# DeltaNet and a PReLU feed-forward on one core: the banks of two solves, one row step, two banks of the ninth chunk and the shape of the last stores

## The chip, the core and the metric

The kernel runs on one core of a Trainium2 chip. Its engines work through their own instruction streams and meet through semaphores: TensorE (PE in the profile) multiplies matrices and writes into PSUM, eight banks of 512 fp32 values per partition; VectorE (DVE) and ScalarE (ACT) read those banks; GpSimd (POOL) computes in SBUF alone; SyncE (SP) issues most DMA transfers. The metric is the device time of one execution in microseconds (us). A profiled execution also has a span, from its first to its last instruction, which is a little shorter.

## The reference

Two blocks follow one another. The first is the delta rule for 4 batches and 8 heads, 768 tokens, 48 dimensions a head:

```python
k_n = k / (np.linalg.norm(k, axis=-1, keepdims=True) + 1e-06)
state = np.zeros((B, H, D, D))
for t in range(S):
    y[:, :, t] = einsum('bhd,bhde->bhe', q[:, :, t], state)
    v_old = einsum('bhde,bhd->bhe', state, k_n[:, :, t])
    state = state + beta_t * einsum('bhd,bhe->bhde', k_n[:, :, t], v[:, :, t] - v_old)
```

Its output, taken as 3072 tokens of 384 values, goes through a feed-forward layer:

```python
h = x @ w_in                                          # 384 -> 2048
g = np.maximum(h, 0.0) + alpha * np.minimum(h, 0.0)
out = g @ w_out                                       # 2048 -> 384
```

All data is fp32. The output array has one row of 384 values (1536 bytes) for each token, batch after batch.

## The kernel before, in words

**Chunks and steps.** The sequence is cut into 12 chunks of 64 tokens (NCH). A step is one chunk of one pair of batches, so there are 24 steps (N), two for each chunk. Within a chunk the recurrence becomes a triangular system: its matrix is made of products of keys (grams), its inverse is found block by block on VectorE (eliminate), and each step then needs a few groups of small matmuls.

**What a step does.** through_state (L801) multiplies the keys with the state and with the queries; the right-hand side r is made of its first part (L825) and the masked matrix a_t of its second (L508). query (L789) multiplies queries and state; ScalarE copies the result as y (L799). between_1 and between_2 (L773, L776, matmuls at L747) make the off-diagonal block of the inverse, with copies by ScalarE (L759). solve (L914, matmuls at L917) multiplies the inverse with r, and VectorE scales it to u (L921). outputs (L926, L930) adds to y (L936), next_state (L940, L946) updates the state (L954). flips (L441, transposes at L430) turn keys and queries of later steps, to_ffn (L962, L969) turns y into the input of the feed-forward layer.

**Banks.** Two banks, p_ffn, belong to the feed-forward layer; until step 15 the other six form three pairs, p_pair. ps_big() (L76) hands out the pairs in turn. From step LATE = 16 on there are two pairs and two more single banks, p_more (L1998); the single banks are then ffn_banks[0] to [3].

**Order of the work.** The instructions of all engines stand in the order in which the program issues them. Steps 4 and 5 are written out in attention (L1454), from step JOINED = 6 on a step is three bursts (burst_a, turn_round, burst_b), each followed by a stretch (L1973) in which weave (L1437) mixes pieces of three streams: the feed-forward layer of earlier chunks (tail), the elimination of later blocks, and small work put off. Each stream gets positions evenly spread between its starting point and 1: the feed-forward pieces from 0, the pieces of the elimination from 0.3. How many of each a stretch takes stands in FILL and PIECES_OF (L1989 to L1995) for steps 6 to 8. A piece of the elimination in its middle part is a row step, one multiply (L565) and one add (L571) on VectorE, from 30 to 240 elements wide.

**The feed-forward layer.** Chunks 2 to 7 take w_in in ffn_in (L1066): groups of matmuls (L1075) into the two p_ffn banks in turn, then a relu on ScalarE (L1085) and two instructions on VectorE (L1087) that free the bank. Their w_out is done by ffn_out_fast (L1128) as seven products of half size, each ended by an add on VectorE (L1160). The ninth chunk (FAST_IN = 8, counted from 0) is the first to take ffn_in_fast (L1262) and ffn_out_faster (L1367): eight pairs of columns, each with its own bank of ffn_banks[0] to [2] and its shared products in p_more, then seven products again, in a list of banks at L1397.

**Stores.** store (L1098) writes the 128 rows of an o_sb tile, 32 for each batch, to four places of the output, one transfer a batch, on SyncE's queue; in the last chunk every other one goes on ScalarE's. The last chunk stores three times: half of the tokens in full rows of 1536 bytes, then the left halves of the others (768 bytes), and, behind the last product and its add (L1425), their right halves. Then the program waits for all transfers (L2069).

Of the kernel before, what the change touches and what calls it, by code (L numbers as in the profile page):

```python
# [32 lines left out]
C = 64  # L33
# [5 lines left out]
FAST_IN = 8  # L39
# [4 lines left out]
def kernel(  # L44
# [11 lines left out]
    nc = tc.nc  # L56

    B, H, S, D = q.shape
    DM = H * D
    DFF = moe_w_in.shape[1]  # L60
    NCH = S // C
# [12 lines left out]
    doubles, big, ffn_banks = ExitStack(), [], []  # L74

    def ps_big():  # L76

        big.append(big.pop(0))
        return big[-1]
# [211 lines left out]
    for t in range(2):  # L291
# [7 lines left out]
        out=quarter_of, in_=ident.rearrange("p (t q e) -> p q t e", t=2, q=NQ4),  # L299
# [11 lines left out]
        out=picked, in0=minus.rearrange("p (q c) -> p q c", c=LB),  # L311
# [154 lines left out]
    def now(pieces):  # L466
        for x in pieces:
            x()
# [628 lines left out]

    def store(c, u, o_sb, cols=slice(0, DM)):  # L1098

        for b in range(B):  # L1100
            tok = b * S + c * C + 32 * u
            queue = nc.scalar if c == NCH - 1 and b % 2 else nc.sync
            queue.dma_start(out=out[tok : tok + 32, cols], in_=o_sb[32 * b : 32 * b + 32, cols])

    def ffn_out(c, together=False):

# [155 lines left out]
    def ffn_in_fast(c):  # L1262
        xt = xts[c]
        gss[c] = [act_of(c, i) for i in range(FP)]
        due = due_of[c] = Due()
        t = spare()[2]

        def x(k, u):
            return xt[:, k, u * 128 : (u + 1) * 128]

        def quarter(flat):
            return flat.rearrange("p (i e) -> p i e", e=128)

        def terms(i):

            if i % 2 == 0:
                return spare()[1]
            if "block" not in held:
                held["block"] = work.tile([128, HB * (HB + 1)], FP32, name="block", bufs=1)
            return quarter(held["block"][:, 0:512])  # L1280

        def pair(i):
            p = ffn_banks[i % 3]
            q = quarter(ffn_banks[2 if i == 0 else 3])
            z, g = terms(i), act_of(c, i)
            if "less" not in held:
                held["less"] = work.tile([128, G, 128], FP32, name="k_t", bufs=EARLY + 1)
            r = held["less"] if i % 2 == 0 else quarter(held["block"][:, 512:1024])
            r = r.rearrange("p (f u) e -> p f (u e)", f=2)

            def w(k, f):
                return w_in[:, k, (2 * i + f) * 128 : (2 * i + f + 1) * 128]

            def s(x):
                return input_sum(x, i // 4)[:, i % 4]

            def whole(f):
                nc.tensor.matmul(  # L1298
                    p[:, f * 256 : f * 256 + 256], w(2, f), xt[:, 2], start=True, stop=False
                )  # L1300

            def more(j, a, b):
                nc.tensor.matmul(  # L1303
                    p[:, j * 128 : j * 128 + 128], a, b, start=False, stop=(j > 0)
                )

            def shared(j, a, b):
                nc.tensor.matmul(q[:, j], a, b, start=True, stop=True)  # L1308

            def own():  # L1310
                whole(0)
                yield
                more(0, w(1, 0), x(1, 0))
                more(1, w(0, 1), x(1, 1))
                yield
                whole(1)
                yield
                more(2, w(1, 1), t[:, 3])
                yield

            def common():
                shared(0, w(0, 0), x(0, 0))
                shared(1, s(1), t[:, 1])
                yield
                shared(2, s(2), t[:, 2])
                shared(3, s(0), t[:, 0])
                nc.scalar.copy(z, q)  # L1327
                for dst, a, b in (
                    (z[:, 1], z[:, 0], z[:, 1]), (z[:, 2], z[:, 1], z[:, 2]),
                    (z[:, 1::2], z[:, 1:3], z[:, 3:4].to_broadcast([128, 2, 128])),  # L1330
                ):
                    nc.gpsimd.tensor_tensor(out=dst, in0=a, in1=b, op=ALU.add)  # L1332
                yield

            def total():
                h = g.rearrange("p f i -> p (f i)")
                nc.vector.tensor_tensor(
                    out=h, in0=p, in1=z.rearrange("p i e -> p (i e)"), op=ALU.add
                )

            def below():
                nc.scalar.activation(r, g, ACT.Relu, scale=-1.0)  # L1342

            def slope():
                for f in range(2):
                    nc.vector.scalar_tensor_tensor(  # L1346
                        out=g[:, f], in0=r[:, f], scalar=al_t[:, 2 * i + f : 2 * i + f + 1],
                        in1=g[:, f], op0=ALU.mult, op1=ALU.add,
                    )

            due.put(PER * (i + 1) + {0: PER, FP - 1: 2}.get(i, 3), total)
            due.put(PER * (i + 2) + {FP - 2: 1, FP - 1: -4}.get(i, 2), below)
            due.put(PER * (i + 2) + {FP - 2: 1, FP - 1: -2}.get(i, 5), slope)
            for gen in (own(), common()) if i == 0 else (common(), own()):
                for _ in gen:
                    due.step()
                    yield

        early = operand_sums(0)
        due.put(PER * 6 + 5, lambda: next(early, None))  # L1360
        rest = chain(early, operand_sums(1))
        for at in (6, 6, 7, 7, 8, 9, 10):
            due.put(PER * FP + at, lambda: next(rest, None))
        for i in range(FP):
            yield from pair(i)

    def ffn_out_faster(c):  # L1367

        gss.pop(c)
        due = due_of.pop(c)  # L1370
        o = [work.tile([128, DM], FP32, name="o_sb") for _ in range(2)]
        left, right_ = slice(0, DM // 2), slice(DM // 2, DM)
        u = [work.tile([128, DM // 2], FP32, name=f"u{i}", bufs=1) for i in (2, 3)]

        def operand(f, u):
            return lambda i: act[:, i, f, u * 128 : (u + 1) * 128]

        def sum_(x):
            return lambda i: sums[:, i, x]

        def weight(f, v):
            return lambda i: w_half[:, i, f, v]

        def w_sum_(x):
            return lambda i: w_sum(i, x)

        def add(to, x, p):
            nc.vector.tensor_tensor(out=to, in0=x, in1=p, op=ALU.add)

        def some(p, x, w, which):  # L1390
            for i in which:
                nc.tensor.matmul(p, x(i), w(i), start=(i == 0), stop=(i == FP - 1))  # L1392
                if i % 2 == 1:
                    due.step()
                    yield

        p = [ffn_banks[i][:, 0 : DM // 2] for i in (3, 2, 0, 3, 2, 1, 3)]  # L1397
        a = (p[0], operand(0, 0), weight(0, 0))
        b = (p[1], operand(1, 0), weight(1, 0))
        yield from some(*a, range(FP - 2))  # L1400
        yield from some(*b, range(FP - 2))
        yield from some(*a, range(FP - 2, FP))
        nc.scalar.copy(u[0], p[0])
        yield from some(*b, range(FP - 2, FP))
        add(o[0][:, left], u[0], p[1])
        yield from some(p[2], operand(1, 1), w_sum_(3), range(FP))
        assert not due.left
        yield from some(p[3], sum_(1), w_sum_(1), range(FP))
        add(u[0], u[0], p[3])
        yield from some(p[4], lambda i: act[:, i, 0, 128:256], w_sum_(2), range(FP))  # L1410
        add(u[1], u[0], p[4])
        add(o[1][:, left], u[1], p[2])
        yield from some(p[5], sum_(0), w_sum_(0), range(FP))
        add(o[0][:, right_], u[0], p[5])
        add(o[1][:, right_], u[1], p[5])
        store(c, 1, o[1])
        last = c == NCH - 1
        if last:
            store(c, 0, o[0], left)
        yield from some(p[6], sum_(2), weight(1, 1), range(FP - 2))  # L1420
        if c + 1 < NCH:
            assert c + 1 in whole
            token_sums(c + 1)
        yield from some(p[6], sum_(2), weight(1, 1), range(FP - 2, FP))
        add(o[0][:, right_], o[0][:, right_], p[6])  # L1425
        store(c, 0, o[0], right_ if last else slice(0, DM))
# [27 lines left out]
    def attention(n):  # L1454
# [2 lines left out]
        now(through_state(n))  # L1457
        now(between_1(n + 1))
        yield
        now(solve(n))  # L1460
        now(grams(n + EARLY))
        now(between_2(n + 1))
# [517 lines left out]
    for n in range(NJ, JOINED):  # L1980
# [7 lines left out]
    assert next(late, None) is None  # L1988
    PIECES_OF = {  # L1989
        JOINED: (3, WHOLE - 2 * PIECES - 6 - 2 * share - 3, 2 * PIECES),  # L1990
        JOINED + 1: (0, 4, 7), JOINED + 2: (4, 5, 5),
    }
    TURNS = [(3, 3, 4), (3, 3, 4), (4, 4, 4), (0, 5, 6)]
    FILL = {JOINED: (8, 12, 12), JOINED + 1: (10, 12, 10), JOINED + 2: (8, 10, 12)}
# [79 lines left out]
```

## Time and profile before

| | |
|---|---|
| runs shown | 646.87, 647.69, 648.09 us (median 647.69) |
| profiled execution | 648.95 us |
| its span | 647.2 us |
| granted TensorE clock | 0.997 |
| TensorE busy | 635.0 us (98%) |
| VectorE busy | 482.9 us (75%) |
| ScalarE busy | 258.6 us (40%) |
| written to memory | 4.72 MB |
| issue to landing of a store, median | 1.6 us |

A line of the timeline gives the start in us, the duration, the engine with the line of the kernel, the operation, the tile it writes and the tiles it reads, the shapes and the number of instructions merged; in brackets stand the idle time before it and what ended it. SPq and ACTq are the issues of DMA transfers on SyncE's and ScalarE's queues: the time is that of the issue, not of the data. In the view of the DMA queues each queue has its packets, its megabytes and the time its packets took as a share of 16 engines over the window.

### The profile page before, as it was taken

What the parts mean: (1) busy time and instruction counts of PE and PEld (TensorE: products, weight loads), DVE (VectorE), ACT (ScalarE), POOL (GpSimd) and SP (SyncE); (2) the same over time, 40 slices, a digit from 0 to 9 for tenths busy, and PEclk for the clock granted to TensorE, in tenths of its full rate; (3) what the DMA queues carried; (4) which work ended last, traced back from release to release, by engine and by line L of the source; (5) the groups of instructions that cost most, each with busy time, mean ns of one, the idle gap of its engine ahead of it and who ended that gap; (6) DMA issues with size and microseconds to landing.
All of it is one profiled execution on the core that took longest, in us unless ns stands there. A gap on an engine that the chain in (4) does not pass through costs nothing.

```text
span 647.2 us, 21391 instructions
## 1 busy us (share of the span) xinstructions
PE 635.0 (98%) x9177; PEld 562.7 (87%) x9177; DVE 482.9 (75%) x1160; ACT 258.6 (40%) x605; POOL 125.3 (19%) x248
## 2 busy tenths in 40 slices
PE   8899999999999999999999999999999999999997
PEld 7677787567889989989989989989999999999997
DVE  5858689978998788578678577678868568477383
ACT  6667664245553253254154144034045054042240
POOL 7267610010001000000000010000044053062360
PEclk9989999999999999999999999999999999999999
DMA  8668755113511320311210211211221210100000
GB/s 131 169 160 240 208 129 129 23 29 64 99 25 29 76 50 3 69 37 23 60 27 17 46 32 26 41 40 22 43 42 19 54 23 2 39 2 3 25 0 26
DMA packets 106799, 36.89 MB, mean 57 GB/s; under 512 B 99872, under 2 KB 103088, under 8 KB 106704
## 3 DMA queue, kind: packets, MB, share of 16 engines
q1 hardware_dynamic: 104832, 35.03, 25.0%
q8 instruction: 72, 1.18, 0.8%
q10 hardware_dynamic: 1872, 0.49, 0.4%
q14 instruction: 23, 0.19, 0.1%
HBM read 30.78 MB, written 4.72 MB: 55 GB/s over the span
## 4 chain that ended last, share of the span: by engine, by line
PE 86%; DVE 8%; issue 2%; ACT 2%; POOL 1%; DMA 1%; SPq 0%; POOLq 0%; DVEq 0%; ACTq 0%
PE p_ffn L1075 24%; PE p_ffn L1140 17%; PE p_more L1392 8%; PE p_more L1308 5%; PE p_ffn L1118 4%; PE p_ffn L1298 3%; PE p_ffn L1392 3%; PE p_ffn L1303 2%; PE p_pair L430 2%; PE p_pair L807 2%; PE p_pair L747 2%; PE p_pair L486 2%; PE p_pair L930 2%; PE p_pair L917 2%; PE p_pair L795 1%
## 5 line engine op out<-in xcount | busy, mean ns | idle before, releaser
L1075 PE MATMUL p_ffn<-xt,w_in 128*128 128x256 f32 x768 | 177.5, 384 | 0.7 <-DVE act L1087 0.5
L1075 PEld LDWEIGHTS p_ffn<-xt,w_in 128*128 128x128 f32 x768 | 142.0, 190 | 21.5 <-issue 1.5
L1085 ACT ACTIVATE act<-p_ffn 128x512 f32<-128x512 f32 x56 | 33.3, 595 | 80.4 <-PE p_ffn L1075 80.2
L1087 DVE SCALAR_TENSOR_TENSOR act<-act,al_t,p_ffn 128x256 f32<-128x256 f32 x112 | 48.5, 474 | 20.0 <-ACT act L1085 19.7
L1332 POOL TENSOR_TENSOR k_t<-k_t 128x128 f32<-128x128 f32 (+1 forms) x48 | 29.9, 623 | 167.5 <-ACT k_t L1327 165.0
L571 DVE TENSOR_TENSOR block<-block,prod 128x30 f32<-128x30 f32 (+9 forms) x150 | 50.0, 333 | 5.2
L565 DVE TENSOR_TENSOR prod<-block 128x30 f32<-128x30 f32 (+9 forms) x150 | 49.0, 327 | 4.2 <-POOL block L555 2.7
L419 POOL TENSOR_TENSOR beta_t<-beta_t,rec 128x8 f32<-128x8 f32 x20 | 5.1, 257 | 235.2 <-DVE rec L413 219.3
L1140 PE MATMUL p_ffn<-w_out,act 128*128 128x192 f32 x288 | 49.6, 328 | 0.0
L973 ACT COPY xt<-p_pair 128x384 f32<-128x384 f32 x22 | 10.4, 478 | 91.2 <-PE p_pair L969 77.5
L1140 PEld LDWEIGHTS p_ffn<-w_out,act 128*128 128x128 f32 x288 | 46.6, 190 | 0.3
L1332 POOL TENSOR_TENSOR block<-block 128x128 f32<-128x128 f32 (+1 forms) x48 | 28.0, 583 | 16.0 <-ACT block L1327 13.5
L1298 PE MATMUL p_ffn<-xt,w_in 128*128 128x256 f32 x96 | 28.7, 381 | 0.5 <-DVE o_sb L1160 0.5
L759 ACT COPY inv<-p_pair 32x256 f32<-32x256 f32 x40 | 14.5, 361 | 24.9 <-DVE u L921 24.1
L1160 DVE TENSOR_TENSOR o_sb<-u,p_ffn 128x192 f32<-128x192 f32 x24 | 7.9, 351 | 20.5 <-PE p_ffn L1140 20.0
L799 ACT COPY y<-p_pair 128x384 f32<-128x384 f32 x22 | 10.5, 479 | 31.1 <-PE p_pair L795 29.5
L1346 DVE SCALAR_TENSOR_TENSOR act<-block,al_t,act 128x256 f32<-128x256 f32 x32 | 19.1, 638 | 4.7 <-ACT block L1342 4.7
L1327 ACT COPY k_t<-p_more 128x512 f32<-128x512 f32 x16 | 9.4, 587 | 31.7 <-PE p_more L1308 27.9
L825 DVE TENSOR_TENSOR r<-v_raw,p_pair 64x192 f32<-64x192 f32 (+1 forms) x60 | 21.2, 353 | 1.0
L1392 PE MATMUL p_more<-w_out,act 128*128 128x192 f32 x128 | 21.9, 329 | 0.0
L1118 PE MATMUL p_ffn<-w_out,act 128*128 128x384 f32 x64 | 21.7, 490 | 0.0
L921 DVE TENSOR_TENSOR u<-p_pair,wgt 128x384 f32<-128x384 f32 x20 | 11.1, 555 | 14.0 <-PE p_pair L747 14.0
(286 smaller groups left out, 1424.1 us busy)
## 6 DMA issues: line engine op xcount, KB each, us to landing
v_raw<-in_v_dram SPq DMA_DIRECT2D x48, 96.0 KB, 3.1
qp<-in_q_dram SPq DMA_DIRECT2D x48, 96.0 KB, 3.1
out_dram<-o_sb SPq DMA_DIRECT2D x90, 48.0 KB, 1.6
space_out<-in_moe_w_out_dram SPq DMA_DIRECT2D x11, 384.0 KB, 4.0
ke<-in_k_dram SPq DMA_DIRECT2D x43, 96.0 KB, 3.4
kl<-in_k_dram SPq DMA_DIRECT2D x80, 48.0 KB, 2.7
w_out<-in_moe_w_in_dram SPq DMA_DIRECT2D x6, 512.0 KB, 5.1
w_out<-in_moe_w_out_dram SPq DMA_DIRECT2D x5, 384.0 KB, 5.9
```

The lines of the kernel that those rows point to most:

```text
L565: nc.vector.tensor_tensor(out=prod, in0=r[:, 0:j, j : j + 1].to_broadcast([128, j, n]), in1=r[:, j : j + 1, j + 1 : HB].to_broadcast([128, ...
L571: nc.vector.tensor_tensor(out=r[:, 0:j, j + 1 : HB], in0=r[:, 0:j, j + 1 : HB], in1=prod, op=ALU.add)
L825: nc.vector.tensor_tensor(out=r[to, a], in0=v_in[to, a], in1=p[own, a, :, 0:D], op=ALU.subtract)
L1075: nc.tensor.matmul(p_h[:, i], w_in[:, t, (f + i) * 128 : (f + i + 1) * 128], xt[:, t], start=(t == 0), stop=(t == KT - 1),)
L1085: nc.scalar.activation(g, p_h, ACT.Relu, scale=-1.0)
L1087: nc.vector.scalar_tensor_tensor(out=g[:, i], in0=g[:, i], scalar=al_t[:, f + i : f + i + 1], in1=p_h[:, i], op0=ALU.mult, op1=ALU.add,)
L1118: nc.tensor.matmul(p_o[u], gs[f // 2][:, f % 2, u * 128 : (u + 1) * 128], w_out[:, f], start=(f == 0), stop=(f == FT - 1),)
L1140: nc.tensor.matmul(p, x(i), w(i), start=(i == 0), stop=(i == FP - 1))
L1298: nc.tensor.matmul(p[:, f * 256 : f * 256 + 256], w(2, f), xt[:, 2], start=True, stop=False)
L1308: nc.tensor.matmul(q[:, j], a, b, start=True, stop=True)
L1332: nc.gpsimd.tensor_tensor(out=dst, in0=a, in1=b, op=ALU.add)
L1392: nc.tensor.matmul(p, x(i), w(i), start=(i == 0), stop=(i == FP - 1))
```

## The change

There are four edits. In attention, so at steps 4 and 5, one more turn of ps_big() stands ahead of the solve: it writes the pair that the query used, and every later pair moves by one. In step 8 the first stretch takes three row steps in place of four and the second six in place of five. In the ninth chunk the two banks p_ffn0 and p_ffn1 change places, for the pairs of ffn_in_fast and for the third and the sixth product of ffn_out_faster. In the last chunk a store is two transfers in place of four, one a queue, each with the rows of two batches; in the other chunks it is what it was.

```diff
     def store(c, u, o_sb, cols=slice(0, DM)):
 
+        rows = out.rearrange("(b s) d -> b s d", b=B)[:, c * C + 32 * u : c * C + 32 * u + 32, cols]
+        if c == NCH - 1:
+            for i, queue in enumerate((nc.sync, nc.scalar)):
+                queue.dma_start(out=rows[2 * i : 2 * i + 2], in_=o_sb[64 * i : 64 * i + 64, cols])
+            return
         for b in range(B):
-            tok = b * S + c * C + 32 * u
-            queue = nc.scalar if c == NCH - 1 and b % 2 else nc.sync
-            queue.dma_start(out=out[tok : tok + 32, cols], in_=o_sb[32 * b : 32 * b + 32, cols])
+            nc.sync.dma_start(out=rows[b], in_=o_sb[32 * b : 32 * b + 32, cols])
...
         def pair(i):
-            p = ffn_banks[i % 3]
+            p = ffn_banks[(i, 10 - i)[c == FAST_IN] % 3]
...
-        p = [ffn_banks[i][:, 0 : DM // 2] for i in (3, 2, 0, 3, 2, 1, 3)]
+        x, y = (1, 0) if c == FAST_IN else (0, 1)
+        p = [ffn_banks[i][:, 0 : DM // 2] for i in (3, 2, x, 3, 2, y, 3)]
...
         now(through_state(n))
         now(between_1(n + 1))
         yield
+        ps_big()
         now(solve(n))
...
-        JOINED + 1: (0, 4, 7), JOINED + 2: (4, 5, 5),
+        JOINED + 1: (0, 4, 7), JOINED + 2: (3, 6, 5),
```

## The prediction

> **What bounds the kernel.** I read the page first, then every idle stretch of TensorE, then the last microseconds.
>
> ```profile
> PE 635.0 (98%) x9177; PEld 562.7 (87%) x9177; DVE 482.9 (75%) x1160; ACT 258.6 (40%) x605; POOL 125.3 (19%) x248
> ...
> PE 86%; DVE 8%; issue 2%; ACT 2%; POOL 1%; DMA 1%; SPq 0%; POOLq 0%; DVEq 0%; ACTq 0%
> ```
>
> TensorE sets the end. From 90 us on it stands idle for more than 0.12 us at only four places of the trace: 141.93 (0.50), 164.92 (0.19), 239.24 (0.48) and 468.93 (0.54). Three of them, and the tail behind the last matmul, are where the change works. Time taken from TensorE elsewhere would arrive at the end unless another engine is late by an absolute time; each VectorE idle stretch between 150 and 240 us ends on TensorE's work or on ScalarE work that follows it, so a shift of TensorE shifts VectorE too.
>
> **Steps 4 and 5.** The solve's bank (timeline at step 4):
>
> ```profile
> 140.08 1.08 DVE L825 TENSOR_TENSOR r<-v_raw,p_pair 128x192 f32<-128x192 f32 x3
> ...
> 141.19 0.69 DVE L508 TENSOR_TENSOR a_t<-p_pair,minus 128x512 f32<-128x512 f32 x1
> ...
> 141.93 0.68 PE L917 MATMUL p_pair<-r,inv 64*64 64x48 f32 x32 [0.50 <-DVE a_t L508]
> ```
>
> The solve writes the bank pair that through_state filled, so it waits for a_t (ends 141.88), though its operand r is ready at 141.15. The extra ps_big() gives it the query's pair, which ScalarE's copy of y freed at 139.22. TensorE's matmuls before it end at 141.43, and a 64-row group starts some 0.07 before such an end, so the solve starts at 141.36: **−0.57**. r is then 0.2 early and is the next to be late. At step 5 the solve starts at 155.68, freely it would be 155.62: **−0.06**. What follows rotates by one: grams takes between_1's pair (copied by 140.09, used at 141.9), between_2 takes through_state's (a_t at 141.88, used at 142.45); neither waits. Outputs needs u, which ends at 144.42 in VectorE's fixed order and is wanted at 145.2. At step 5 u ends only 0.1 before its use; VectorE starts 0.57 earlier there (it idles 2.1 until 152.11), so it just holds. The two extra turns also shift which pair is oldest when the pool is remade at step 16; the last copy out of any old pair ends at 401.7, the new ones are written from 406.9: nothing.
>
> **The ninth chunk.** Timeline at its start:
>
> ```profile
> 468.42 0.36 DVE L1160 TENSOR_TENSOR o_sb<-u,p_ffn 128x192 f32<-128x192 f32 x1 [0.91 <-PE p_ffn L1140]
> ...
> 468.93 0.67 PE L1298 MATMUL p_ffn<-xt,w_in 128*128 128x256 f32 x2 [0.54 <-DVE o_sb L1160]
> ```
>
> Its first pair writes the bank of the product that has just ended (468.39) and waits for its add. The other bank was emptied at 465.41 and the token sums end at 466.95. Such a start lies 0.16 before the end of the product (the tenth chunk's: product to 516.18, start at 516.02): 468.23 in place of 468.93, **−0.70**. The exchanged banks come round again at the tenth chunk: its first pair then follows the sixth product, whose adds end at 513.47, and is wanted at 516.02. No new wait.
>
> **The row step of step 8** (VectorE, between steps 8 and 9):
>
> ```profile
> 216.88 0.38 DVE L565 TENSOR_TENSOR prod<-block 128x220 f32<-128x220 f32 x1
> 217.29 0.39 DVE L571 TENSOR_TENSOR block<-block,prod 128x220 f32<-128x220 f32 x1
> 220.21 0.35 DVE L1160 TENSOR_TENSOR o_sb<-u,p_ffn 128x192 f32<-128x192 f32 x1 [2.53 <-PE p_ffn L1140]
> ...
> 223.86 0.86 DVE L1087 SCALAR_TENSOR_TENSOR act<-act,al_t,p_ffn 128x256 f32<-128x256 f32 x2
> 224.64 0.55 DVE L921 TENSOR_TENSOR u<-p_pair,wgt 128x384 f32<-128x384 f32 x1
> ...
> 228.61 0.87 DVE L1087 SCALAR_TENSOR_TENSOR act<-act,al_t,p_ffn 128x256 f32<-128x256 f32 x2 [2.00 <-ACT act L1085]
> ...
> 239.24 0.89 PE L1075 MATMUL p_ffn<-xt,w_in 128*128 128x256 f32 x3 [0.48 <-DVE act L1087]
> ```
>
> Weaving the shares by hand: the second stretch (10 pieces of feed-forward) has its first row step before the add at 220.21 and the others behind it, all ahead of L1087. With 4 and 5 steps, four stand behind the add; with 3 and 6, five do. The extra one is the 220-element step, 0.38 + 0.39 and two gaps of 0.03: 0.84. It leaves a place ahead of 2.53 idle and enters a chain without a hole: add 220.21, row steps, L1087, u (ends 225.19), ScalarE's copies L759 (they start 0.03 behind u), L700, L725, L700, relu L1085 at 227.98 (its matmuls ended about 227.3), L1087 at 228.61, then VectorE busy without idle to 239.10, for which TensorE waits at 239.24. So **+0.84**; at zero, if the chain had slack that I don't see. The stall that stands there now is cured by steps going the other way.
>
> **The last stores.** Timeline and queues of the end (641 to 648 us):
>
> ```profile
> 643.82 0.35 DVE L1388 TENSOR_TENSOR o_sb<-o_sb,p_more 128x192 f32<-128x192 f32 x1 [1.98 <-PE p_more L1392]
> 644.20 0.78 SPq L1103 DMA_DIRECT2D out_dram<-o_sb  x2
> 644.20 0.85 ACTq L1103 DMA_DIRECT2D out_dram<-o_sb  x2
> ...
> q10 hardware_dynamic: 288, 0.20, 10.5%
> q1 hardware_dynamic: 288, 0.20, 10.5%
> ```
>
> Twelve transfers become six; six DMA issues of 0.31 to 0.44 go, three a queue. Four lie beside the last product (both queues are done at 643.68, before 644.20); only the second pair, from 644.56 and 644.62, is on the path. If nothing else changed, the end would gain the 0.41 between the two issues, less some 0.17 for twice the rows behind one another, less up to 0.28 if an issue with two counts takes 0.60 as the two-count key loads do (0.595 at the least, against 0.315): 0.0 to −0.3, and −0.1 by those loads.
>
> But the shape changes too. Of each queue's 288 packets 192 are rows and 96 are end writes of 4 bytes: 16 for each of 6 transfers. All 354 transfers of the trace end with 16, and all have an outermost count of 16, 32, 64 or 128. The new one has batches outermost: 2 x 32 rows. No row shows how such a transfer is dealt to the 16 engines. One end is all 16, the other one engine a batch, two in all. I take **two**: every row fits a transfer cut along its outermost count, each a multiple of 16, and the nearest is the 16-row load of the slopes, one row for each end write; a cut by rows fits too, so this is a choice and not a reading. Then both queues send all rows through the same two engines, if nothing tells their transfers apart. In the packet records a 1536-byte row takes 62 ns (fastest tenth; mean 92 in this burst), a 768-byte row 36 ns (median; fastest 34, mean 40). One engine's work is 64 x 0.062 + 128 x 0.036 = 8.6, from the first packet at 642.68 to 651.3, where the last packet now ends at 645.85: **+5.4**. With the fastest rows +5.2; with this burst's share of the queues, 2 x 10.5% x 16 x 7 us = 23.5 engine-us over two engines, 654.4: +8.6.
>
> The Trainium skill (DMA: Bandwidth & Descriptors, "Why a DMA increments its semaphore by 16 and not by 1") says that a transfer is cut along the slowest dimension over one and the largest number of engines up to 16 that divides both sides' counts, and takes the lowest-numbered ones; by that rule 2 and 64 give two engines, shared by both queues. No run here shows it yet.
>
> **Sum.** −0.57 − 0.06 − 0.70 + 0.84 + 5.4 = +4.9. The profiled execution took 648.95 (span 647.19 and 1.76 around it): 653.9. The runs' median, 647.69, is 1.26 below that execution; I forecast 647.69 + 4.9 = **652.6**, own range 651.5 (row step free, fastest rows) to 655.8 (mean row times).
>
> **Rivals**, in the medians' frame:
> - *All 16 engines.* The end gains 0.1, the sum is −0.6: 647.1, not slower. For it: nothing in the trace shows fewer than 16 engines. Against: no count of 2 occurs. It decides at the engines' number: with n shared engines the first 12.5 engine-us end at 642.68 + 12.5/n and the last 4.6/n follow, not before 645.0. The other terms' −0.49 is eaten when the last row comes after 646.34, which is so from four engines down (646.96), not at five (646.1). Chance 0.14. The Trainium skill (same page, "Rules for kernel authors") advises to coalesce small transfers; by that advice this case would win.
> - *Each queue has its own two engines* (four in all): +1.1 at the end, +0.6 in all: 648.3. Chance 0.10.
> - *All 16, and the row step is hidden* because the chain from 220.2 to 239.2 has slack: −1.4: 646.3, faster. Against it: no idle over 0.1 in that chain but the 2.0 that ScalarE's order makes. Chance 0.05.
> - *The change doesn't do what it says*: the solve still waits, for y's copy instead. It ended 2.7 us before; under 0.01, kept with a rest of 0.01 for anything slower.
>
> The forecast has 0.70. The range 648.0 to 655.8 holds it and the four-engine case, 0.80. This kernel's measurement can tell about 0.2%, 1.3 us, from no change: faster (below 646.4) 0.05, same 0.24 (the first two rivals), slower 0.71.
>
> **What would show it.** The solve of step 4 without its idle, at 141.4; L1298 of the ninth chunk right behind L1140; the wait at L1075 near 239 grown to about 1.3, perhaps in two parts; the last VectorE add some 0.5 earlier than 643.82, and behind it no longer 1.7 us of stores but about 8, at a DMA share near 2/16, with 2 end writes a transfer in place of 16. If the last add comes early and the DMA view ends within 2 us of it, the stores' step is wrong; if the wait near 239 stays at 0.5, the row step's.

## The result, and the profile after

The changed kernel takes **654.26 us** (median of 6 runs, 653.21 to 655.76), the kernel before 647.89 beside it (6 runs): a ratio of **1.0095, interval 1.0072 to 1.0118**, slower by 6.4 us. The profiled execution took 654.23 us, with a span of 652.5 us and a granted clock of 0.994.

TensorE does no more work than before. The first view is the page of the changed kernel: the engines' busy time, and the chain that ended last.

```profile
PE 631.4 (97%) x9177; PEld 559.4 (86%) x9177; DVE 484.2 (74%) x1160; ACT 258.4 (40%) x605; POOL 124.5 (19%) x248
...
PE 84%; DVE 7%; DMA 3%; POOL 2%; issue 2%; ACT 1%; SPq 1%; POOLq 0%; DVEq 0%; ACTq 0%
```

DMA stood at 1% of the chain and stands at 3%. In the timeline the waits at step 4 and at the start of the ninth chunk are gone. First step 4, then the ninth chunk (L1143 was L1140 before the change, L1301 was L1298, L1163 was L1160, L1391 was L1388, L1395 was L1392):

```profile
139.89 0.69 DVE L508 TENSOR_TENSOR a_t<-p_pair,minus 128x512 f32<-128x512 f32 x1
...
140.05 0.68 PE L917 MATMUL p_pair<-r,inv 64*64 64x48 f32 x32
```

```profile
465.79 1.63 PE L1143 MATMUL p_ffn<-w_out,act 128*128 128x192 f32 x9
...
467.25 0.59 PE L1301 MATMUL p_ffn<-xt,w_in 128*128 128x256 f32 x2
467.45 0.35 DVE L1163 TENSOR_TENSOR o_sb<-u,p_ffn 128x192 f32<-128x192 f32 x1 [0.89 <-PE p_ffn L1143]
```

The solve starts while a_t is still being written, without idle time in brackets; L1301 starts 0.17 before the product ends and ahead of its add. The row step's place shows two waits at L1075 where there was one of 0.48 (timeline of step 8):

```profile
218.40 0.35 DVE L1163 TENSOR_TENSOR o_sb<-u,p_ffn 128x192 f32<-128x192 f32 x1 [2.75 <-PE p_ffn L1143]
...
233.45 2.83 PE L1075 MATMUL p_ffn<-xt,w_in 128*128 128x256 f32 x12 [0.36 <-DVE act L1087]
...
238.27 1.97 PE L1075 MATMUL p_ffn<-xt,w_in 128*128 128x256 f32 x8 [0.49 <-DVE act L1087]
```

The end, from the timeline, and the stores in the view of the DMA queues from 641 to 653 us:

```profile
640.11 2.85 SPq L1103 DMA_DIRECT2D out_dram<-o_sb  x3
640.11 2.85 ACTq L1103 DMA_DIRECT2D out_dram<-o_sb  x3
642.06 0.35 DVE L1391 TENSOR_TENSOR o_sb<-o_sb,p_more 128x192 f32<-128x192 f32 x1 [1.98 <-PE p_more L1395]
```

```profile
DMA  0110110201111111111111111111111110000000
...
q1 hardware_dynamic: 198, 0.20, 6.1%
q10 hardware_dynamic: 198, 0.20, 4.6%
```

A queue has 198 packets where it had 288: the 192 rows and 6 end writes in place of 96, two for each transfer. From the last add on (ends at 642.41) to the last packet (651.12) the share of the 16 engines stays low; in the window's own row it is 0.13, near 2/16:

```profile
642.41:651.50 9.09, 0.00 (x0) 0.00 (x0) 0.00 (x1) 0.00 (x0) 0.00 (x0) 0.66 0.13 42
```

The columns after the window are its length, the five engines' busy time, the granted clock, the DMA share and GB/s. No engine works in it. These 8.71 us were 1.68 before (last add to 644.17, last packet to 645.85): **+7.0**.

**Where each part of the time went.** The table follows the same TensorE instructions through both traces: start after minus start before.

| up to | difference, us | what lies between |
|---|---|---|
| 112 us | −1.31 | no edit |
| past steps 4 and 5 | −1.84 | solves: −0.57 and −0.06; +0.09 comes back at L946 of step 5 |
| past step 8 | −0.97 | row step: +0.84; +0.03 near 193 us |
| past the ninth chunk's start | −1.75 | exchanged banks: −0.70 at the first matmul, −0.78 from the second on |
| end of the last add | −1.76 | nothing |
| last packet | +5.27 | stores: +7.0 |

From 112 us on the parts sum to −0.57 − 0.06 + 0.09 + 0.03 + 0.84 − 0.78 + 7.0 = +6.6, where the medians differ by 6.4. The −1.3 of the first 112 us lies ahead of every edit; in the executions below the same stretch differs by −1.3 to +2.6 from the profiled execution of before, so it is taken as a difference between executions.

### The profile page after: what moved, and what is told of

It reads as the page before. It is cut to its first block, busy times and chain, and to the rows that moved or that the text cites. A ratio compares the mean times of both kernels' runs of the same rounds, so it can differ in the third digit from the quotient of the medians.

```text
span 652.5 us, 21390 instructions
## 1 busy us (share of the span) xinstructions
PE 631.4 (97%) x9177; PEld 559.4 (86%) x9177; DVE 484.2 (74%) x1160; ACT 258.4 (40%) x605; POOL 124.5 (19%) x248
## 4 chain that ended last, share of the span: by engine, by line
PE 84%; DVE 7%; DMA 3%; POOL 2%; issue 2%; ACT 1%; SPq 1%; POOLq 0%; DVEq 0%; ACTq 0%
PE p_ffn L1075 23%; PE p_ffn L1143 17%; PE p_more L1395 8%; PE p_ffn L1121 5%; PE p_more L1311 5%; PE p_ffn L1301 3%; PE p_ffn L1395 3%; PE p_ffn L1306 2%; PE p_pair L747 2%; PE p_pair L807 2%; PE p_pair L430 2%; PE p_pair L930 2%; PE p_pair L917 2%; DMA ke<-in_k_dram 2%; PE p_pair L486 1%
## 5 line engine op out<-in xcount | busy, mean ns | idle before, releaser
L1075 PE MATMUL p_ffn<-xt,w_in 128*128 128x256 f32 x768 | 177.8, 384 | 2.9 <-ACT w_in L240 1.5
L1075 PEld LDWEIGHTS p_ffn<-xt,w_in 128*128 128x128 f32 x768 | 141.9, 190 | 24.2 <-issue 2.2
L1087 DVE SCALAR_TENSOR_TENSOR act<-act,al_t,p_ffn 128x256 f32<-128x256 f32 x112 | 48.5, 473 | 19.9 <-ACT act L1085 19.7
L1143 PE MATMUL p_ffn<-w_out,act 128*128 128x192 f32 x288 | 49.6, 328 | 0.0
L1143 PEld LDWEIGHTS p_ffn<-w_out,act 128*128 128x128 f32 x288 | 46.5, 190 | 0.3
L973 ACT COPY xt<-p_pair 128x384 f32<-128x384 f32 x22 | 10.4, 478 | 91.2 <-PE p_pair L969 77.5
L1301 PE MATMUL p_ffn<-xt,w_in 128*128 128x256 f32 x96 | 28.7, 380 | 0.0
L1163 DVE TENSOR_TENSOR o_sb<-u,p_ffn 128x192 f32<-128x192 f32 x24 | 7.9, 350 | 20.7 <-PE p_ffn L1143 20.3
L1395 PE MATMUL p_more<-w_out,act 128*128 128x192 f32 x128 | 21.9, 329 | 0.0
L807 PE MATMUL p_pair<-beside,k_t 48*64 48x112 f32 x704 | 21.4, 259 | 0.2 <-ACT beside L458 0.2
```

The costliest lines, as they stand in the source:

```text
L807: nc.tensor.matmul(p[half(t ^ a), a, g], k_t[n][dims(a), g, half(t)], beside[bp][dims(a), t, g])
L1075: nc.tensor.matmul(p_h[:, i], w_in[:, t, (f + i) * 128 : (f + i + 1) * 128], xt[:, t], start=(t == 0), stop=(t == KT - 1),)
L1087: nc.vector.scalar_tensor_tensor(out=g[:, i], in0=g[:, i], scalar=al_t[:, f + i : f + i + 1], in1=p_h[:, i], op0=ALU.mult, op1=ALU.add,)
L1301: nc.tensor.matmul(p[:, f * 256 : f * 256 + 256], w(2, f), xt[:, 2], start=True, stop=False)
```

## The experiments

Theory A is the prediction's: a transfer with two batches outermost uses two engines, the same two for both queues, and that is nearly all of the loss; the banks gain 1.3, the row step loses 0.8. The rivals are that the loss comes from elsewhere (the issues, or the move of rows as such), and that the row step costs nothing. Each time below is the median of 4 to 12 executions, and each ratio is against executions of the kernel before made beside them.

### The changed kernel with the stores of before

```diff
-        rows = out.rearrange("(b s) d -> b s d", b=B)[:, c * C + 32 * u : c * C + 32 * u + 32, cols]
-        if c == NCH - 1:
-            for i, queue in enumerate((nc.sync, nc.scalar)):
-                queue.dma_start(out=rows[2 * i : 2 * i + 2], in_=o_sb[64 * i : 64 * i + 64, cols])
-            return
         for b in range(B):
-            nc.sync.dma_start(out=rows[b], in_=o_sb[32 * b : 32 * b + 32, cols])
+            tok = b * S + c * C + 32 * u
+            queue = nc.scalar if c == NCH - 1 and b % 2 else nc.sync
+            queue.dma_start(out=out[tok : tok + 32, cols], in_=o_sb[32 * b : 32 * b + 32, cols])
```

> The changed kernel with the stores of before: four transfers a store in the last chunk, one a batch; the other three edits stay. Theory A (a transfer is dealt to as many DMA engines as its outermost count allows, so the new stores ran on two): the tail behind the last VectorE add shrinks from 8.7 us to the 1.7 us of before, each transfer ends with 16 end writes, and the kernel takes 7.0 us less than the changed one: 0.5 us below the kernel before, ratio 0.999. Rival B (the new stores cost only the 5.4 us that were forecast, and 1 us of the loss is in the other three edits): about 0.5 us above the kernel before, ratio 1.001. Inside, both expect the solve of step 4 0.65 us earlier, the wait near 239 us 0.9 us longer, the ninth chunk 0.7 us earlier.

Measured: 647.40 us, ratio 0.9981 (0.9969 to 0.9993). In its trace the last packet ends 1.68 behind the last add, with 96 end writes a queue; the other terms stand as in the changed kernel (−0.57 and −0.06, +0.84, −0.70 and then −0.78). Without its stores the change is a small gain: all of the loss is in four lines.

### The kernel before with the new stores alone

```diff
+        rows = out.rearrange("(b s) d -> b s d", b=B)[:, c * C + 32 * u : c * C + 32 * u + 32, cols]
+        if c == NCH - 1:
+            for i, queue in enumerate((nc.sync, nc.scalar)):
+                queue.dma_start(out=rows[2 * i : 2 * i + 2], in_=o_sb[64 * i : 64 * i + 64, cols])
+            return
...
```

> The kernel before with the new stores alone. Theory A: 7.0 us more than before, ratio 1.0108, two end writes a transfer and rows one behind another at 0.061 us (1536 bytes) and 0.036 us (768 bytes) on each of two engines. Rival B (part of the loss is in the other edits): 5.4 us more, ratio 1.0083.

Measured: 655.94 us, ratio 1.0107 (1.0078 to 1.0137). The last add ends at 644.15, as in the profiled execution of before (644.17), so these two can be laid side by side:

| | before | new stores | forecast |
|---|---|---|---|
| first store's issue | 641.86 | 641.85 | |
| first packet | 642.68 | 643.11 | 642.68 |
| last packet | 645.85 | 652.93 | 651.3 |
| behind the last add | 1.68 | 8.78 | 7.1 |
| end writes a queue | 96 | 6 | 6 |

From the first packet to the last the packet records show exactly two packets open in 8.3 of the 9.8 us and never more than four (before: up to 18). In the middle of a burst two long rows start in every 61 ns and each takes 65, so each of the two engines works off its rows one behind another. The two queues don't start together: SyncE's first row comes at 643.11, ScalarE's at 646.24, which is 4.39 after its issue (before: 642.68 and 642.91).

### All four batches in one transfer, on one queue

```diff
+        rows = out.rearrange("(b s) d -> b s d", b=B)[:, c * C + 32 * u : c * C + 32 * u + 32, cols]
+        if c == NCH - 1:
+            nc.sync.dma_start(out=rows, in_=o_sb[:, cols])
+            return
...
```

> The kernel before, but a store of the last chunk is one transfer of all four batches (4 x 32 rows) on SyncE's queue. Theory A: four engines, one queue. One engine's work is 32 x 0.061 for the full rows and 2 x 32 x 0.036 for the halves, and the right halves, issued at 644.2, cannot end before about 646.6, with the slow first rows of the changed kernel 648.0: 0.8 to 2.2 us more than before, ratio 1.001 to 1.0035, 4 end writes a transfer. Rival C (a transfer with two counts, or with more rows, is slow whatever the number of engines, since its rows are made one after another): 384 rows through one queue, none beside another, at least as slow as the changed kernel: 7 us or more, ratio 1.011 or above. Rival D (16 engines after all): 0.3 us less.

Measured: 650.95 us, ratio 1.0027 (1.0008 to 1.0046), with 4 end writes a transfer and four packets open for most of the time; the last packet comes 4.0 behind the last add. The window of its end, from the last add's end on (columns as above):

```profile
644.26:648.60 4.34, 0.00 (x0) 0.00 (x0) 0.00 (x0) 0.00 (x0) 0.00 (x0) 0.81 0.24 84
```

The share is 0.24, near 4/16, where two batches gave 0.13. Twice as much in a transfer, half as many transfers, one queue in place of two, and it is faster by 5 us: the outermost count sets the number of engines. Four engines cost 2.3 behind the last add, where the rival with four engines was worked out at 1.1.

### Tokens outermost, two batches' worth of rows a transfer

The o_sb tile is laid out token by token, so that a transfer has 16 tokens outermost and 4 batches within.

```diff
-        rows = out.rearrange("(b s) d -> b s d", b=B)[:, c * C + 32 * u : c * C + 32 * u + 32, cols]
+        rows = out.rearrange("(b s) d -> s b d", b=B)[c * C + 32 * u : c * C + 32 * u + 32, :, cols]
...
-                queue.dma_start(out=rows[2 * i : 2 * i + 2], in_=o_sb[64 * i : 64 * i + 64, cols])
+                queue.dma_start(out=rows[16 * i : 16 * i + 16], in_=o_sb[64 * i : 64 * i + 64, cols])
...
-            nc.sync.dma_start(out=rows[b], in_=o_sb[32 * b : 32 * b + 32, cols])
+        nc.sync.dma_start(out=rows, in_=o_sb[:, cols])
...
-                dst = xts[c].rearrange("p k (u b t i) -> p b k u t i", u=2, b=NB, t=2)[:, bp]
+                dst = xts[c].rearrange("p k (u i b t) -> p b k u t i", u=2, b=NB, t=2)[:, bp]
```

> The changed kernel with the tokens of a half chunk laid out token by token (all four batches of a token beside one another) in place of batch by batch: the copy into the input of the feed-forward layer writes every fourth column, a store of the last chunk is again one transfer a queue of 64 rows, but its outermost count is 16 tokens, with 4 batches inside; the other chunks store with one transfer of 32 tokens x 4 batches. Theory A: 16 engines again, 16 end writes a transfer, the tail 1.4 to 1.7 us, so the time of the changed kernel less 7.0 to 7.3 us: 0.5 to 0.8 us below the kernel before, ratio 0.999. Rival C (two counts or 64 rows in one transfer are slow by themselves): the tail stays at 7 us or more, ratio 1.009. If the copies with a step of four columns are slower, both would see it in the copies' duration, 0.48 us before.

Measured: 648.82 us, ratio 0.9998 (0.9983 to 1.0013). Here a transfer of 64 rows has 16 end writes, and the stores are as short as before: the DMA row from 641 to 655 us, in 40 slices, where one digit 9 is nearly all engines at once.

```profile
DMA  0000000049640005200000000000000000000000
```

The last packet comes 1.81 behind the last add, against 1.68: with all engines kept, six transfers are no better than twelve. At the last store a queue has one issue of 0.54 or 0.55 in place of two, 0.32 and 0.42 on SyncE's. But the first packet comes 1.20 after the issue in place of 0.82 (+0.38), and only 0.25 of it is won back from there to the last packet (0.58 in place of 0.83). The rest of the gain of the banks went elsewhere: ScalarE now scatters the transposed y in steps (L973), which takes nearly twice as long. First its group in before, then here (busy time and mean ns of one behind the bar):

```profile
L973 ACT COPY xt<-p_pair 128x384 f32<-128x384 f32 x22 | 10.4, 478 | 91.2 <-PE p_pair L969 77.5 <-DVE o_sb L1160 13.6
```

```profile
L973 ACT COPY xt<-p_pair 128x384 f32<-128x384 f32 x22 | 19.0, 872 | 91.3 <-PE p_pair L969 77.5 <-DVE o_sb L1162 13.6
```

Between 160 and 168 us TensorE has two waits that before doesn't have: 0.17 at 160.16 for u (L921, VectorE) and 0.25 at 167.40 for ScalarE's copy L725. Neither is for the longer copy itself. L725 stands behind it on ScalarE, and so do L408 and L409, for which VectorE waits before it makes r and u. In all TensorE loses 0.24 here between 158 and 200 us against the changed kernel.

### The row step alone

```diff
-        JOINED + 1: (0, 4, 7), JOINED + 2: (4, 5, 5),
+        JOINED + 1: (0, 4, 7), JOINED + 2: (3, 6, 5),
```

> The kernel before with the row steps of step 8 as (3, 6, 5) and nothing else. Theory A: TensorE loses 0.84 to 0.9 us between 234 and 240 us, in two waits for the feed-forward banks, and nothing elsewhere: ratio 1.0014. Rival B (slack in the chain hides it, and the loss seen in the changed kernel comes from TensorE being 0.65 us early): no loss, ratio 1.000.

Measured: 649.48 us, ratio 1.0007 (0.9986 to 1.0028); the times alone can't tell this from no change. The trace can: TensorE is later by 0.60 at the first matmuls behind 236.45 and by 0.24 more at 239.69, **0.84** in all, and nowhere else behind 112 us.

```profile
236.45 2.83 PE L1075 MATMUL p_ffn<-xt,w_in 128*128 128x256 f32 x12 [0.36 <-DVE act L1087]
...
241.26 1.97 PE L1075 MATMUL p_ffn<-xt,w_in 128*128 128x256 f32 x8 [0.49 <-DVE act L1087]
```

The first line is the new wait, for a bank of the feed-forward layer. The second is the old one of 0.48, which costs no more than before. The other 0.24 is lost between them at the transposes L430, which start right behind a_t (L508) on VectorE.

### The banks alone, and with the row step moved the other way

The first kernel is the changed one with the stores and the row steps of before, the second has (5, 4, 5) row steps in place of (4, 5, 5).

```diff
-        JOINED + 1: (0, 4, 7), JOINED + 2: (3, 6, 5),
+        JOINED + 1: (0, 4, 7), JOINED + 2: (5, 4, 5),
```

> The solves' banks and the exchange in the ninth chunk alone; row steps (4, 5, 5) and stores as before. Theory A (the three edits act each at its own place and add): solve of step 4 and 5 -0.65 us, ninth chunk -0.70, the wait near 239 us as before (0.48 shown as idle): 1.35 us below the kernel before, ratio 0.9979. Rival B (the moved row step mends something that the solves' banks open, so that it is needed beside them): a new wait in steps 6 to 9 and less than 0.7 us of gain.

> The solves' banks and the exchange in the ninth chunk, stores as before, and a row step of step 8 moved the other way: (5, 4, 5). Theory A: the chain from the add near 220 us to the wait near 239 gets one row step of 0.87 us shorter, so that wait (0.65 us with what belongs to it) goes: -0.65 -0.70 -0.65 = 2.0 us below the kernel before, ratio 0.997. Rival B (the step's place does not matter): 1.35 below, ratio 0.998.

Measured: 647.26 us, ratio 0.9973 (0.9957 to 0.9989), and 647.44 us, ratio 0.9973 (0.9953 to 0.9994). The banks gain what was worked out: in both traces −0.57 at step 4 and −0.70 at the first matmul of the ninth chunk, −0.78 from the second on. But the step moved back gains next to nothing (0.05 at 237.8). The prediction had said that the stall near 239 "is cured by steps going the other way"; it isn't. In the timeline of (5, 4, 5):

```profile
224.07 0.56 DVE L921 TENSOR_TENSOR u<-p_pair,wgt 128x384 f32<-128x384 f32 x1 [0.28 <-PE p_pair L747]
...
238.68 4.67 PE L1075 MATMUL p_ffn<-xt,w_in 128*128 128x256 f32 x20 [0.49 <-DVE act L1087]
```

VectorE is early, and waits ahead of u: 0.35 at L1087 for ScalarE's relu, then 0.28 at u (L921) for TensorE. With (4, 5, 5) u has no such wait, with (3, 6, 5) VectorE comes there some 0.85 later. So u is the place where the two engines meet, and the 0.49 belongs to what VectorE has to do behind u.

### A row step taken from behind u

To test that, a step is taken from the third stretch, which lies behind u, and put into the first: (5, 5, 4). The banks are as changed and the stores as before.

```diff
-        JOINED + 1: (0, 4, 7), JOINED + 2: (4, 5, 5),
+        JOINED + 1: (0, 4, 7), JOINED + 2: (5, 5, 4),
```

> The banks of the two solves and of the ninth chunk as changed, the stores as before, and step 8 with (5, 5, 4) row steps in place of (4, 5, 5): the step is taken from the third stretch, which lies behind u (L921). Theory A, from the two runs before this one: the wait of 0.49 at L1075 near 238 belongs to what VectorE does between u and that wait, since with (5, 4, 5) VectorE merely waited for TensorE ahead of u and the wait kept its 0.49. So with one row step less (0.8) behind u and one more ahead of it, in front of 2.5 idle, the wait goes: TensorE gains 0.5 near 238 against banks_only, 0.5 less than before's time - 0.57 - 0.70 at the end, a ratio of 0.9965 or so. Rival B: the wait hangs on ScalarE's order behind u or on another engine; then it keeps 0.49 and the time is that of banks_only, 0.9973. Rival C: the extra step ahead of u makes u late; then a new wait of up to 0.8 stands near 226 and the ratio is 0.998 to 0.999.

Measured: 645.95 us, ratio **0.9965 (0.9948 to 0.9982)**, the lowest ratio here. Its timeline has no wait at that place, and none over 0.2 anywhere behind 90 us:

```profile
226.76 0.55 DVE L921 TENSOR_TENSOR u<-p_pair,wgt 128x384 f32<-128x384 f32 x1
...
240.62 2.59 PE L1075 MATMUL p_ffn<-xt,w_in 128*128 128x256 f32 x11
```

TensorE gains 0.70 there against before, and u is as late against TensorE as with (4, 5, 5), so the third rival falls too. That it is faster than the banks alone the times don't show, since the two intervals overlap; the trace does.

### The new stores in four chunks

The edit stands against the kernel before with the new stores alone.

```diff
-        if c == NCH - 1:
+        if c >= FAST_IN:
             for i, queue in enumerate((nc.sync, nc.scalar)):
-                queue.dma_start(out=rows[2 * i : 2 * i + 2], in_=o_sb[64 * i : 64 * i + 64, cols])
+                (queue if c == NCH - 1 else nc.sync).dma_start(out=rows[2 * i : 2 * i + 2], in_=o_sb[64 * i : 64 * i + 64, cols])
             return
```

> The kernel before, with the two-batch transfers in chunks 9 to 12 (counted from 1) and not in the last alone; in chunks 9 to 11 both go on SyncE's queue, in the last as in the change. Theory A: a transfer of two batches goes through two engines wherever it stands, with two end writes, and costs only what lies behind the last add: the ratio of before_new_stores, 1.0107, give or take 0.002, and the same 8.7 us of stores behind the last add. In the earlier chunks 128 rows of 1536 bytes take some 4 us (64 rows one behind another on each of two engines at 0.061) beside matmuls, and nothing waits for them. Rival: what goes through those two engines beside them, or the o_sb tiles held longer, stops the next chunk: then 1.012 or more, with a wait of TensorE or VectorE in chunks 10 to 12 that before does not have. It also shows whether the first rows of such a transfer are slow (0.1 to 0.44 each, as in the last chunk) wherever it stands.

Measured: 656.35 us, ratio 1.0110 (1.0083 to 1.0137), against 1.0107 with the new stores in the last chunk alone. In chunks 9 to 11 the rows of a chunk's two stores take about 9 us (515.7 to 524.8, 562.6 to 571.9, 605.9 to 615.2 in the packet records), and TensorE has no wait there that before doesn't have. The estimate of 4 us was for 128 rows; each of these chunks stores 256. The same slow transfers that cost 7 us at the end cost nothing in the middle.

## Why the prediction was right or wrong

**The stores: right in kind, too small.** The prediction took two engines, shared by both queues, for +5.4. Two end writes a transfer, two open packets and a share of 0.13 show two engines; 4 and 16 with outer counts of 4 and 16 show that the count sets them. The rivals of 16 engines and of two engines a queue fall. The Trainium skill (DMA: Bandwidth & Descriptors, "Why a DMA increments its semaphore by 16 and not by 1") has the rule of the slowest dimension, and the three shapes tried here agree with it: 2, 4 and 16 end writes. The Trainium skill's advice to coalesce small transfers (same page, "Rules for kernel authors", where another row warns of an outermost count below 16) did not pay in any shape tried here: +7.0 us with two engines, +2.3 with four (4.0 behind the last add in place of 1.68) and +0.13 with sixteen.

The step that was mis-sized is "64 x 0.062 + 128 x 0.036 = 8.6, from the first packet at 642.68 to 651.3". The 36 ns of the short rows held. Two things did not. The first packet came at 643.11, not 642.68: 1.26 after the issue, where a transfer of one count needs 0.82 (**+0.43**). And the work of one engine took 9.82 instead of 8.6 (**+1.2**): most long rows take 65 ns and start 61 apart, but the first rows of a burst are slow. In the first store the rows, both engines' in order of time, took 69, 108, 256, 114, 316, 386, 439, 424 and then mostly 65 ns. Seven more rows of 0.12 to 0.39 us follow up to 646.4. All of them belong to the first transfer on SyncE's queue: its 64 long rows sum to 7.1 engine-us in the records. ScalarE's 64 take 65 ns each, 4.2 in all, and every short row takes 36. So the slow rows add 3.0 engine-us, some 1.5 on each engine, enough for the 1.2 that the term lacked. The fastest rows, which the prediction took for its likeliest value, hold for every later transfer, but not for the first.

**The saving of issues.** The prediction gave it 0.0 to 0.3 if the engines stayed. It is not there: with all engines the tail is 0.13 longer. The step that failed is that it put the later first packet of a two-count transfer (+0.38) at nothing; no store of before had shown one.

**Steps 4 and 5**: −0.57 and −0.06 forecast and measured at the two solves. But 0.09 of it comes back at next_state of step 5 (L946), in every trace with the new banks (0.09 to 0.11). There the prediction had said that VectorE "just holds": VectorE is only 0.54 earlier, TensorE 0.63, and L946 waits for VectorE's L494. It starts 0.64 behind the outputs (L930), where it was 0.55 before and is 0.50 at the steps around it. **Ninth chunk**: −0.70 forecast, −0.70 measured at its first matmul. From the second on it is −0.78, since the second followed the first by 0.29 behind the wait and follows it by 0.22 without one.

**The row step**: +0.84 forecast, +0.84 measured alone and within the change. Its place is not quite the one that was named: the wait near 239 does not grow, it stays at 0.49; 0.60 is lost at a new wait at L1075 some 5 us earlier and 0.24 at L430. That there was no slack ahead of u is shown by the step moved back, which only makes VectorE wait ahead of u. The prediction's remark on the cure was wrong, as told above: the chain of 234 to 240 is closed through TensorE at u, and only work taken from behind u shortens it.

**The sum**: +4.9 forecast, +6.4 by the medians; the difference is that of the stores' term (+7.0 for +5.4), and nothing else is off by more than 0.1. That the slow first packet and the slow first rows fell inside the range is partly luck: its upper end came from the mean row times of a burst on sixteen engines, not from either of them.

What stays open: why ScalarE's first row comes 4.4 us after its issue with two batches a transfer, and why the first rows of a burst on few engines are slow. The slow rows don't come from the two queues, since the transfer of four batches on SyncE's queue alone has rows of up to 399 ns too; nor from the end of the kernel, since the stores of chunks 9 to 11 begin with 69, 107, 245, 116 to 124, 292 to 301, 368 to 376, 371 and 276 to 286 ns each time. With 16 engines and tokens outermost the median of the first stores is 65 and the longest is 101.

## What to carry to other kernels

Merging transfers is safe only if the outermost count of the merged shape still spreads it over all engines: look at that count, and at the number of end writes in the packet records, before counting the issues saved; with all engines kept it gained nothing here. A transfer on few engines cost nothing beside other work (chunks 9 to 11) and cost in full behind the last instruction, so the last stores are the worst place to try it. Where a wait closes a loop between two engines, find the instruction at which they meet and take work away behind it; work moved ahead of that place only changes which engine waits there.

## What the runs showed of the hardware that was not expected

- In the last chunk the issue of a store with two counts takes 0.50 to 0.68 us (once 0.83) against 0.31 to 0.44 with one. In the three kernels with two batches a transfer ScalarE's first issue, at the same moment as SyncE's, takes 1.36; with 16 tokens outermost it takes 0.60.
- From the issue of a two-count store on SyncE's queue to its first packet it is 1.15 to 1.28 us in five kernels, against 0.82 for one count. ScalarE's first packet comes 4.4 to 4.7 after its issue with two batches a transfer, 1.5 with 16 tokens outermost and 1.05 before.
- On one DMA engine long rows (1536 bytes) start 61 ns apart and short ones (768 bytes) take 36, once a burst runs. On two engines the first eight rows of a burst take up to 0.44 us each, in nearly the same pattern in every chunk, and single slow rows follow for some microseconds.
- Elsewhere in the kernel the 1536-byte rows of the stores take 80 ns at the median with 32 tokens of one batch a transfer and 65 with 32 tokens of four batches, on 16 engines both times.
- A ScalarE copy of 128x384 from PSUM takes 478 ns, and 872 when it writes every fourth value.
